# Decays of a chunkwise recurrence by half chunks, and a first product in two column parts

## Chip, cores, metric

One core of a Trainium2 chip. The metric is device time in microseconds of one execution of the kernel; the median of three runs stands for it.

## The reference

Four batches of eight heads run a gated recurrence over 768 steps with head size 40, and two dense layers follow it. Cut to what matters:

```python
for t in range(S):
    m_new = np.maximum(f_gate[:, :, t] + m, i_gate[:, :, t])
    f_stab = np.exp(f_gate[:, :, t] + m - m_new)
    i_stab = np.exp(i_gate[:, :, t] - m_new)
    C = f_stab * C + i_stab * outer(vt, kt)
    n = f_stab * n + i_stab * kt
    y[:, :, t] = sigmoid(o_gate) * (C @ qt) / max(abs(n @ qt), 1)
x = y as (3072 tokens, 320)
h = x @ w_in;  g = h - tanh(h);             x = g @ w_out
h = x @ w_in;  g = h, 0 or (h + 1)**2 / 4;  return g @ w_out
```

Each layer has 2048 hidden columns. Everything is float32.

## The kernel before

The recurrence is computed in chunks of 128 steps (L). A job n is one chunk of one batch: n = 4 * chunk + batch, so there are 24 jobs. For its eight heads, in two halves u of four heads, a job forms:

- d, the decay matrix: for every pair of steps (s, t) of the chunk the product of f over the steps between. VectorE makes it for a half with one tensor_tensor_scan (line 462) of 128x512: data0 is f of the four heads, broadcast over partitions, with a 0 at each head's first step; data1 is scan_id, the identity four times. For jobs 0 to 3 the broadcast is made by TensorE (t_f, line 453); from job 4 on (FIRST) it is a load, fb, from the scratch tensor fr_d.
- the scores k times q (t_s, line 475, and line 493 from job 12 on), and their product with d on VectorE (line 497).
- t_n: q times the carried state C (line 524) plus d times V (line 533). V is scaled by i on GpSimd (line 504), K by the last column of d, copied by ScalarE into wc (lines 465, 510).
- the output x: t_n over its denominator, times the output gate (lines 540 to 558), three transposes t_x on TensorE (line 562) and the copy into the layer's operand (xf for jobs 0 to 3, line 598).
- the new state: K times V (t_c, line 569), and C (line 586).

The gates run for all 32 heads at once in five groups of chunks. `decays` finishes a group: the running product gr (line 389), a 0 at each chunk's first step (line 392), and the writes of f and gr to scratch memory.

The layers work on blocks of four jobs, 512 tokens. A step is one of 16 groups of 128 hidden columns: first product (line 651 for steps 0 to 7 of block 0, in plain f32 and called wide; line 661 else), activation, second product (line 713). Steps of one block and jobs of the next are interleaved. The weights of layer 1 arrive as 64-bit words and are rebuilt by ScalarE and VectorE (lines 322 to 335).

The order on every engine is made by a planner, the class Plan. Each operation has an engine, a cost, a priority and the buffers that it reads and writes; a list scheduler sets the order, and each engine then runs its instructions in that order. Where the planner sees TensorE idle ahead of step 0 it puts in filler products into a spare bank (line 807). The operations that the prediction follows are these:

```python
op("DVE", dve(1024), p, lambda o=dk[u][0], i=f[u][0]: nc.vector.tensor_tensor_scan(
    out=o(), data0=i(), data1=scan_id, initial=0.0, op0=ALU.mult, op1=ALU.add), [f[u][1], "scan_id"], [dk[u][1]], lock=n >= FIRST)
```

Of the kernel before, what the change touches and what calls it, by code (L numbers as in the profile page):

```python
# [18 lines left out]
L = 128  # L19
# [18 lines left out]
FIRST = BLK[0]  # L38

# [10 lines left out]
WIDE = 8  # L50
W_LATE = 15
# [24 lines left out]
class Plan:  # L76
# [10 lines left out]
    def __init__(self):  # L87
        self.ops, self.tags, self.last, self.read = [], {}, {}, {}
        self.warm, self.end_warm, self.filler, self.gate, self.more = True, None, None, None, {}
# [33 lines left out]
    def schedule(self):  # L123
# [32 lines left out]
        while done < len(self.ops):  # L156
# [44 lines left out]
            done += 1  # L201
        self.ops.sort(key=lambda o: (o.start, o.seq))
# [30 lines left out]
def mlstm_moe_moe(ctx: ExitStack, tc: tile.TileContext, ig, fg, qk, qk3, q3, nat, w1, w2, cst, out):  # L233
# [11 lines left out]
    scan_bf = scan_id.bitcast(BF16)  # L245
# [5 lines left out]
    fr_d = dram.tile([NC, B * H, L], F32, name="fr_d")  # L251
# [129 lines left out]
    def decays(g, prio):  # L381
# [5 lines left out]
        for c in range(cb - ca):  # L387
            if ca + c:
                op("DVE", dve(2 * L), prio + 0.1 * c, lambda c=c: nc.vector.tensor_tensor_scan(
                    out=gr[:, c * L:(c + 1) * L], data0=fr[0:32, c * L:(c + 1) * L], data1=zero, initial=1.0,  # L390
                    op0=ALU.mult, op1=ALU.add), [(fr, c), "zero"], [gr])
            op("DVE", 60, prio + 0.1 * c, lambda c=c: nc.vector.memset(fr[0:32, c * L:c * L + 1], 0.0), [(fr, c)], [(fr, c)])
        z = slice(n - L, n)
        load(max(prio, -60), lambda: fr_d[cb - 1], lambda: fr[0:32, z], 16, [(fr, cb - ca - 1)], [("fr_d", g)], rows=512)
        load(max(prio, -60), lambda: gr_d[cb - 1], lambda: gr[:, z], 16, [gr], [("gr_d", g)], rows=512)
# [12 lines left out]
    def job(n, at, ld):  # L408
# [15 lines left out]
        f = {}  # L424
        if n >= FIRST:
            for u in range(2):
                ft = abuf("fb", [128, HU, L], F32, 2)
                load(ld + 0.5, lambda ft=ft: ft.t.rearrange("p h t -> p (h t)"), lambda u=u: fr_d[
                    c, b * H + u * HU:b * H + (u + 1) * HU].rearrange("h t -> (h t)").unsqueeze(0).to_broadcast([128, HU * L]),
                    256, r=[("fr_d", kc)], w=[ft], rows=512, margin=1200 if n >= 8 else 0.0)  # L430
                f[u] = lambda ft=ft: ft.t.rearrange("p h t -> p (h t)"), ft
# [12 lines left out]
        dk = {}  # L444
        d0 = wbuf(6 + n % 2, [128, 1024], F32, "d0") if n < FIRST else None
        wc = abuf("wc", [128, H], F32, 2)
        for u in range(2):
            p = at(0) if u == 0 else at(1)
            if n < FIRST:
                ft = jbank(n, "f", "t_f")  # L450
                for h in range(HU):
                    r = b * H + u * HU + h
                    op("PE", 2 * pe(L, 128, 2), p, lambda h=h, r=r, ft=ft: nc.tensor.matmul(  # L453
# [490 lines left out]
```

## Time and profile before

| what | value |
|---|---|
| median of 3 runs | 807.09 us (806.79 to 807.47) |
| the profiled execution | 807.17 us, span 805.4 us |
| TensorE busy | 798.4 us, 99% of the span |
| VectorE, ScalarE, GpSimd busy | 566.4, 426.3, 145.1 us |
| granted TensorE clock | 1.0 throughout |

The span runs from the first to the last instruction; the rest of the execution lies around it. Busy time is the union of the instructions' records; a product's record can contain waiting, since products are pipelined.

### The profile page before, as it was taken

To read this page: it belongs to the slowest core of one execution; us is meant where nothing else is said; L and a number is where in the kernel's file an instruction comes from. 1 tells how busy PE (TensorE), PEld (TensorE's weight loads), DVE (VectorE), ACT (ScalarE), POOL (GpSimd) and SP (SyncE) were. 2 spreads that over 40 slices of the span, in tenths; PEclk is the share of its full clock that TensorE was granted. 3 is DMA by queue.
4 is the path that set the end of the run, shared out by engine and by line. 5 is a ranking of instruction groups with operands and counts; after the bars stand their busy time and mean duration, and the time that the engine had idled before them with its cause. 6 is when DMAs were issued, how large, how long until landed. Compare 5 with 4: busy or idle time off the path is not lost.

```text
span 805.4 us, 15259 instructions
## 1 busy us (share of the span) xinstructions
PE 798.4 (99%) x6029; PEld 693.3 (86%) x6029; DVE 566.4 (70%) x924; ACT 426.3 (53%) x810; POOL 145.1 (18%) x146
## 2 busy tenths in 40 slices
PE   9999999999999999999999999999999999999998
PEld 7666888888988989898899898888889889898887
DVE  7999998988887897887466674645546465564644
ACT  4966876566586657554455543534435344342533
POOL 3142233213225234332100200200200101000000
PEclk9999999999999999999999999999999999999999
DMA  8979356676668576771543310100100000000000
GB/s 281 326 225 308 104 178 178 180 246 188 174 172 260 163 213 165 228 217 64 145 133 91 93 34 1 40 33 1 47 26 1 33 1 1 33 1 1 34 1 33
DMA packets 47619, 93.66 MB, mean 116 GB/s; under 512 B 4700, under 2 KB 25020, under 8 KB 47548
## 3 DMA queue, kind: packets, MB, share of 16 engines
q1 hardware_dynamic: 47500, 92.66, 38.8%
q8 instruction: 47, 0.77, 0.4%
q14 instruction: 24, 0.20, 0.1%
q10 hardware_dynamic: 48, 0.03, 0.0%
HBM read 78.88 MB, written 13.80 MB: 115 GB/s over the span
## 4 chain that ended last, share of the span: by engine, by line
PE 95%; DVE 2%; DMA 1%; SPq 0%; issue 0%; ACT 0%; POOL 0%; POOLq 0%; DVEq 0%; ACTq 0%
PE a L713 41%; PE h L661 38%; PE h L651 3%; PE t_n L533 2%; PE h L640 2%; PE t_n L524 2%; PE t_s L475 1%; PE t_c L569 1%; PE t_s L493 1%; PE t_x L562 1%; PE t_f L453 1%; PE spare L807 1%; DMA nat<-in_nat_dram 1%; DVE d L462 1%; SPq L287 0%
## 5 line engine op out<-in xcount | busy, mean ns | idle before, releaser
L661 PE MATMUL h<-x,w 128*128 128x512 f32 x1376 | 340.6, 396 | 0.0
L713 PE MATMUL a<-w,gh 128*128 128x320 f32 x1472 | 328.4, 310 | 0.0
L661 PEld LDWEIGHTS h<-x,w 128*128 128x128 f32 x1376 | 251.6, 188 | 55.2 <-issue 6.9
L713 PEld LDWEIGHTS a<-w,gh 128*128 128x128 f32 x1472 | 248.7, 188 | 8.0 <-ACT ob L736 1.8
L713 PE MATMUL a<-w,gl 128*128 128x320 f32 x736 | 228.2, 311 | 0.0
L684 DVE TENSOR_SCALAR g<-h 128x512 f32<-128x512 f32 x96 | 63.6, 684 | 115.9 <-PE h L661 115.9
L686 ACT ACTIVATE g<-g,half 128x512 f32<-128x512 f32 x96 | 66.9, 721 | 136.2 <-DVE g L684 135.7
L713 PEld LDWEIGHTS a<-w,gl 128*128 128x128 f32 x736 | 138.1, 188 | 0.4
L688 DVE TENSOR_TENSOR g<-h,g 128x512 f32<-128x512 f32 x96 | 64.6, 692 | 27.7 <-ACT g L686 26.9
L692 ACT CAST gh<-g 128x512 fp32r<-128x512 f32 x96 | 59.5, 623 | 43.1 <-DVE g L688 39.8
L680 DVE TENSOR_TENSOR h<-h,g 128x512 f32<-128x512 f32 x88 | 60.9, 693 | 26.8 <-ACT g L679 26.3
L679 ACT ACTIVATE g<-h 128x512 f32<-128x512 f32 x88 | 52.6, 598 | 46.6 <-PE h L661 46.2
L693 DVE TENSOR_TENSOR gl<-h,gh 128x512 fp32r<-128x512 f32 x88 | 59.9, 684 | 20.1 <-ACT gh L692 19.1
L777 POOL TENSOR_TENSOR x<-xl,x 128x512 fp32r<-128x512 f32 x18 | 24.8, 1398 | 271.2 <-ACT x L768 270.7
L692 ACT CAST gh<-h 128x512 fp32r<-128x512 f32 x88 | 51.4, 585 | 40.5 <-DVE h L680 25.4
L693 DVE TENSOR_TENSOR gl<-g,gh 128x512 fp32r<-128x512 f32 x96 | 61.9, 686 | 2.9
L462 DVE TENSOR_TENSOR_SCAN d<-fb,scan_id 128x512 f32<-128x512 f32 x40 | 52.8, 1326 | 2.0 <-DMA fb<-fr_d 1.8
L490 POOL TENSOR_TENSOR xf<-qkraw,xf 120x1024 fp32r<-120x1024 f32 x12 | 29.6, 2467 | 79.5 <-ACT xf L488 48.3
L488 ACT ACTIVATE xf<-qkraw,cs 120x512 fp32r<-120x512 f32 x48 | 32.7, 718 | 15.7 <-PE t_s L493 10.7
L497 DVE TENSOR_TENSOR d<-t_s,d 128x512 f32<-128x512 f32 x48 | 31.8, 680 | 4.6 <-PE t_s L493 2.4
L556 POOL TENSOR_TENSOR nat<-nat,dn 128x320 f32<-128x320 f32 x23 | 21.7, 944 | 69.6 <-DVE dn L542 67.7
L322 ACT ACTIVATE cvb<-w,half 128x704 bf16<-128x704 int8 x32 | 29.8, 932 | 2.1 <-DVE w L324 2.1
(105 smaller groups left out, 754.0 us busy)
## 6 DMA issues: line engine op xcount, KB each, us to landing
w<-in_w_dram SPq DMA_DIRECT2D x32, 703.6 KB
nat<-in_nat_dram SPq DMA_DIRECT2D x24, 484.0 KB
qkraw<-in_qk_dram SPq DMA_DIRECT2D x24, 480.0 KB
fb<-fr_d SPq DMA_DIRECT2D x40, 256.0 KB
w_d<-w SPq DMA_DIRECT2D x16, 352.0 KB
w<-w_d SPq DMA_DIRECT2D x16, 352.0 KB
qkraw<-in_qk_dram SPq DMA_DIRECT2D x24, 160.0 KB
xr_d<-xo SPq DMA_DIRECT2D x24, 160.0 KB
```

The lines of the kernel that those rows point to most:

```text
L462: op("DVE", dve(1024), p, lambda o=dk[u][0], i=f[u][0]: nc.vector.tensor_tensor_scan(out=o(), data0=i(), data1=scan_id, initial=0.0, op0=A ...
L488: op("ACT", act(512, 1), at(u - 1), lambda raw=raw, t=t, z=z, cols=cols: nc.scalar.activation(t[:, cols], raw[:, cols], AF.Copy, scale=cs[ ...
L497: op("DVE", dve(512), at(2 + u), lambda p=sp[u], d=dk[u][0]: nc.vector.tensor_tensor(out=d(), in0=p.t, in1=d(), op=ALU.mult), [sp[u], dk[u ...
L661: op("PE", pe(n), prio, lambda i=i, c=c, s=s: nc.tensor.matmul(p[:, :n], w[:, c:c + 128], x[:, s, :n], start=(i == 0 and not layer), stop= ...
L679: op("ACT", act(n), prio + 0.5 - FFN, lambda: nc.scalar.activation(t[:, :n], p[:, :n], AF.Tanh), [p], [t])
L680: op("DVE", dve(n), prio + 0.5 - FFN, lambda: nc.vector.tensor_tensor(out=p[:, :n], in0=p[:, :n], in1=t[:, :n], op=ALU.subtract), [p, t], [p])
L684: op("DVE", dve(n), prio + 0.5 - FFN, lambda: nc.vector.tensor_scalar(t[:, :n], p[:, :n], -1.0, 1.0, op0=ALU.max, op1=ALU.min), [p], [t])
L686: op("ACT", act(n, 1), prio + 0.5 - FFN, lambda: nc.scalar.activation(t[:, :n], t[:, :n], AF.Square, bias=half[:, 0:1], scale=0.5), [t, "h ...
L688: op("DVE", dve(n), prio + 0.5 - FFN, lambda: nc.vector.tensor_tensor(out=t[:, :n], in0=p[:, :n], in1=t[:, :n], op=ALU.max), [p, t], [t])
L692: op("ACT", act(n), prio + 1 - FFN, lambda: nc.scalar.copy(gh[:, :n], y[:, :n]), [y], [gh])
L693: op("DVE", dve(n), prio + 1 - FFN, lambda: nc.vector.tensor_tensor(out=gl[:, :n], in0=y[:, :n], in1=gh[:, :n].bitcast(F32), op=ALU.subtra ...
L713: op("PE", pe(DM) if gl is not None else 2 * pe(DM, 128, 2), prio, lambda A=A, r=r, a=a, c=c, i=i, dt=dt: nc.tensor.matmul(A[:, 0:DM], a[: ...
```

## The change

From job 4 on, the fifth job (n >= FIRST), a half's d is built from half chunks of 64 steps. d of a half is laid out as (second index half, head, 64 columns). One scan of 128x256 makes both diagonal blocks at once: rows 0 to 63 get f of the first half chunk, rows 64 to 127 of the second, and data1 is half_id, the 64x64 identity four times on each half of the rows. ScalarE copies the second diagonal block (rows 64 to 127) to the columns where it belongs, GpSimd sets the rows it leaves to zero, and the block between the halves (rows 0 to 63, later columns) is a GpSimd product of the first block's last column with the running product inside the second half chunk, which `decays` makes with one more scan (pr). So fr_d has three parts per chunk, and fb is loaded in two pieces. half_id is written over scan_id by two GpSimd copies after job 3. Every product of d times V still has 128 rows.

In steps 0 and 1 the three first products are split into columns of jobs 0 to 2 (384) and of job 3 (128). The scores of job 0 are moved behind the first four products of t_f; one filler is added ahead of them.

```diff
@@ decays
+                pr = abuf("pr", [B * H, HL], F32, 1)
+                op("DVE", dve(L), prio + 0.1 * c, lambda m=m: nc.vector.tensor_tensor_scan(
+                    out=pr.t, data0=fr[0:32, m:m + HL], data1=zero[:, 0:HL], initial=1.0,
+                    op0=ALU.mult, op1=ALU.add), [*f, "zero"], [pr])
...
-        load(max(prio, -60), lambda: fr_d[cb - 1], lambda: fr[0:32, z], 16, [(fr, cb - ca - 1)], [("fr_d", g)], rows=512)
+        for u, a in ((0, z), (2, z + HL)):
+            load(max(prio, -60), lambda u=u, a=a: fr_d[cb - 1, u], lambda a=a: fr[0:32, a:a + HL], 8, [(fr, cb - ca - 1)], [("fr_d", g, u)], rows=256)
+        load(max(prio, -60), lambda: fr_d[cb - 1, 1], lambda: pr.t, 8, [pr], [("fr_d", g, 1)], rows=256)
@@ job: loads of fb
-                ft = abuf("fb", [128, HU, L], F32, 2)
...
-                    256, r=[("fr_d", kc)], w=[ft], rows=512, margin=1200 if n >= 8 else 0.0)
+                ft = abuf("fb", [128, 2 * HU * HL], F32, 2)
+                for a, w, kb in ((0, 2, 128), (HL, 1, 64)):
+                    load(ld + 0.5, lambda ft=ft, a=a, w=w: ft[a:a + HL, 0:w * HU * HL].rearrange("p (w x) -> p w x", w=w),
...
@@ job: d
-            op("DVE", dve(1024), p, lambda o=dk[u][0], i=f[u][0]: nc.vector.tensor_tensor_scan(
-                out=o(), data0=i(), data1=scan_id, initial=0.0, op0=ALU.mult, op1=ALU.add), [f[u][1], "scan_id"], [dk[u][1]], lock=n >= FIRST)
+            op("DVE", dve(512), p, lambda o=dk[u][0], i=f[u][0]: nc.vector.tensor_tensor_scan(
+                out=o()[:, 0:HU * HL], data0=i(), data1=half_id, initial=0.0, op0=ALU.mult, op1=ALU.add),
+               [*f[u][1], ("half_id", 0), ("half_id", HL)], [A, Z], lock=True)
+            op("ACT", act(256), p + 0.3, lambda ds=ds: nc.scalar.copy(ds()[HL:128, 1], ds()[HL:128, 0]), [Z], [D_C])
+            op("POOL", 300, p + 0.4, lambda ds=ds: nc.gpsimd.memset(ds()[HL:128, 0], 0.0), [], [Z])
+            op("POOL", pool(256), p + 0.3, lambda ds=ds, i=pb[u][0]: nc.gpsimd.tensor_tensor(
+                out=ds()[0:HL, 1], in0=i(), in1=ds()[0:HL, 0, :, HL - 1:HL].to_broadcast([HL, HU, HL]), op=ALU.mult),
+               [A, pb[u][1]], [D_B], lock=True)
@@ scores of job 0
+            if n == 0:
+                P.more[o] = 1
+                P.behind.append((o, bc[HU - 1]))
@@ step, wide
+            cut = BLK[0] - 1 if f < SPLIT else 0
+            for a, b in ((0, cut), (cut, BLK[0])) if cut else ((0, BLK[0]),):
+                for i in range(3):
+                    op("PE", 2 * pe((b - a) * L, 128, 2), prio, lambda i=i, z=slice(a * L, b * L): nc.tensor.matmul(
+                        p[:, z], w[:, i * 128:(i + 1) * 128].bitcast(F32), x[:, i, z], start=(i == 0), stop=(i == 2)),
+                       [w, *((x, m) for m in range(a, b))], [p])
@@ after jobs(0)
+    for a in (0, HL):
+        op("POOL", 400, JOB0 + 12, lambda a=a: nc.gpsimd.tensor_copy(
+            half_id[a:a + HL].rearrange("p (h t) -> p h t", t=HL), ident[a:a + HL, a:a + HL].unsqueeze(1).to_broadcast([HL, HU, HL])),
+           ["cs"], ["scan_id", ("half_id", a)])
```

Here SPLIT is 2 and HL is 64. The planner orders every later job anew. Three places show it; rows of the change carry its own line numbers.

TensorE, before, from the last transposes of stage 1 to step 0 (t_x is line 562, step 0's products are line 651; six fillers stand ahead of these rows, behind job 3's d times V):

```order
L807 LDWEIGHTS gh
L807 MATMUL spare<-gh 128x512
L562 MATMUL t_x<-cs,x 128x128 x3
L807 LDWEIGHTS gh
L807 MATMUL spare<-gh 128x512
L807 LDWEIGHTS gh
L807 MATMUL spare<-gh 128x512
L807 LDWEIGHTS gh
L807 MATMUL spare<-gh 128x512
L651 MATMUL h<-xf,wf 128x512 x9
```

The same place now, from job 3's d times V (line 575 of the change; t_x is 604, the wide steps are 695):

```order
L575 MATMUL t_n<-nat,d_389 32x41 x32
L695 MATMUL h<-xf,wf 128x384 x3
L604 MATMUL t_x<-cs,x 128x128 x3
L695 MATMUL h<-xf,wf 128x384 x2
L695 MATMUL h<-xf,wf 128x128 x3
L695 MATMUL h<-xf,wf 128x384
L695 MATMUL h<-xf,wf 128x128 x3
L695 MATMUL h<-xf,wf 128x512 x3
```

The nine fillers are gone, and products of steps 0 and 1 stand around the transposes.

GpSimd at the end of stage 1 and at job 4, before (504 scales V, 510 K, 556 the output gate, 514 and 516 q):

```order
L510 TENSOR_TENSOR nat<-nat,wc 128x320 x2
L556 TENSOR_TENSOR nat<-nat,dn 128x320
L514 TENSOR_TENSOR q_632<-q_632,gb 120x256
L516 TENSOR_TENSOR q_632<-q_632,gb 80x128
L504 TENSOR_TENSOR nat<-nat,isT 128x328
```

Now (552 is the old 510, 598 the old 556, 546 the old 504, 556 and 558 the old 514 and 516; 876 makes half_id, 500 is the product and 499 the zeros of job 4):

```order
L552 TENSOR_TENSOR nat<-nat,wc 128x320
L876 COPY scan_id<-cs 64x256 x2
L552 TENSOR_TENSOR nat<-nat,wc 128x320
L598 TENSOR_TENSOR nat<-nat,dn 128x320
L546 TENSOR_TENSOR nat<-nat,isT 128x328
L500 TENSOR_TENSOR d<-fb,d 64x256
L499 MEMSET d 64x256
L556 TENSOR_TENSOR q_638<-q_638,gb 120x256
L499 MEMSET d 64x256
L558 TENSOR_TENSOR q_638<-q_638,gb 80x128
L500 TENSOR_TENSOR d<-fb,d 64x256
```

The copies stand between the scalings of K, and the second half's product of job 4 stands behind q's scaling.

VectorE at job 4, before (613 and 617 split x, 675 the activation, 324 and 326 weights; a scan is printed as SCALAR_TENSOR_TENSOR):

```order
L613 TENSOR_TENSOR x_634<-xf,x_634 128x1024
L462 SCALAR_TENSOR_TENSOR d<-fb,scan_id 128x512 x2
L497 TENSOR_TENSOR d<-t_s,d 128x512 x2
L675 TENSOR_TENSOR gh<-h,g 128x512
L324 TENSOR_TENSOR w_617<-w_617,cvb 128x704
```

Now (495 is the scan, 539 the old 497, 655 the old 613, 719 the old 675, 331, 333 and 342 weights):

```order
L495 SCALAR_TENSOR_TENSOR d<-fb,scan_id 128x256 x2
L539 TENSOR_TENSOR d<-t_s,d 128x512
L333 SCALAR_TENSOR_TENSOR wf<-w_531,wf 128x704
L331 TENSOR_TENSOR w_631<-w_631,cvb 128x704
L333 SCALAR_TENSOR_TENSOR w_631<-w_555,w_631 128x704
L719 TENSOR_TENSOR gh<-h,g 128x512
L342 TENSOR_TENSOR w_723<-w_631,w_723 128x704
L539 TENSOR_TENSOR d<-t_s,d 128x512
L495 SCALAR_TENSOR_TENSOR d<-fb,scan_id 128x256
L655 TENSOR_TENSOR x_660<-xf,x_660 128x1024
```

The scans come ahead of the split of x, and the second half's product with the scores stands five instructions behind the first's.

## Rows read from the trace of the kernel before

**Rows 1.** The page's engines: busy us (share of the span) xinstructions

```profile
PE 798.4 (99%) x6029; PEld 693.3 (86%) x6029; DVE 566.4 (70%) x924; ACT 426.3 (53%) x810; POOL 145.1 (18%) x146
```

**Rows 2.** Windows: length, busy us of PE, PEld, DVE, ACT, POOL, PEclk, DMA, GB/s

```profile
28.00:31.10 3.10, 2.59 (x24) 1.08 (x12) 2.54 (x6) 2.63 (x7) 0.00 (x0) 1.00 1.01 403
...
40.00:120.00 80.00, 80.00 (x735) 61.27 (x733) 74.62 (x120) 55.52 (x112) 25.48 (x26) 1.00 0.65 203
120.00:390.00 270.00, 268.24 (x2509) 240.20 (x2509) 226.30 (x384) 167.37 (x354) 84.86 (x83) 1.00 0.65 183
```

**Rows 3.** Chain of waits, stage 1 to step 0: start us, us, what

```profile
14.04 1.82 PE t_f L453 x16
...
27.36 0.79 PE t_n L533 x64
...
29.38 0.50 DVE x L553
...
30.02 0.52 PE t_x L562 x3
30.54 0.65 PE spare L807 x3
31.19 7.91 PE h L651 x18
```

**Rows 4.** Timeline, job 0: start us, us, engine, instruction, [idle before, releaser]

```profile
4.99 1.61 PE L475 MATMUL t_s<-qkraw 40*128 40x128 f32 x16
...
8.03 2.34 DVE L462 TENSOR_TENSOR_SCAN d<-t_f,scan_id 128x512 f32<-128x512 f32 x2 [0.93 <-PE t_f L453]
```

**Rows 5.** Timeline, end of stage 1, VectorE and GpSimd

```profile
23.41 0.87 DVE L326 SCALAR_TENSOR_TENSOR wf<-w,wf 128x704 int32<-128x704 int32 x1
...
24.00 0.87 POOL L510 TENSOR_TENSOR nat<-nat,wc 128x320 f32<-128x320 f32 x1 [2.59 <-ACT wc L465]
...
25.67 0.48 DVE L558 TENSOR_TENSOR x<-t_n,nat 128x320 f32<-128x320 f32 x1
```

**Rows 6.** Groups by line: xcount | busy us, mean ns | idle before us, releasers

```profile
L462 DVE TENSOR_TENSOR_SCAN d<-fb,scan_id 128x512 f32<-128x512 f32 x40 | 52.8, 1326 | 2.0 <-DMA fb<-fr_d 1.8
...
L524 PE MATMUL t_n<-C,q 120*128 120x123 f32 (+1 forms) x120 | 16.4, 271 | 0.7 <-POOL nat L504 0.7
...
L562 PE MATMUL t_x<-cs,x 128*128 128x128 f32 x72 | 11.8, 273 | 1.4 <-DVE x L558 0.9 <-DVE x L553 0.5
...
L612 ACT CAST x<-t_x 128x256 fp32r<-128x256 f32 x20 | 7.5, 374 | 8.2 <-PE t_x L562 8.1
...
L797 POOL COPY scan_id<-cs 128x512 f32<-128x512 f32 x1 | 0.7, 746 | 1.2 <-DMA cs<-in_cst_dram 1.2
...
L810 POOL MEMSET gh<- 128x512 f32 x1 | 0.5, 524 | 0.3 <-POOLq L931 0.3
...
L389 DVE TENSOR_TENSOR_SCAN gate<-gate,zero 32x128 f32<-32x128 f32 x1 | 0.4, 407 | 0.2 <-issue 0.2
```

**Rows 7.** One line's instructions: xcount, ns min/median/max, first and last start us

```profile
L514 POOL TENSOR_TENSOR q<-q,gb x20: 732/751/1668, 43.0 to 373.6; 120x256 f32<-120x256 f32 x20
...
L510 POOL TENSOR_TENSOR nat<-nat,wc x20: 714/723/868, 10.9 to 305.1; 128x320 f32<-128x320 f32 x20
...
L462 DVE TENSOR_TENSOR_SCAN d<-fb,scan_id x40: 1172/1215/2182, 44.9 to 372.6; 128x512 f32<-128x512 f32 x40
```

**Rows 8.** Timeline, job 5's scans beside GpSimd

```profile
52.70 2.77 DVE L462 TENSOR_TENSOR_SCAN d<-fb,scan_id 128x512 f32<-128x512 f32 x2
...
52.87 1.52 POOL L556 TENSOR_TENSOR nat<-nat,dn 128x320 f32<-128x320 f32 x1 [3.70 <-DVE dn L542]
```

**Rows 9.** Timeline, jobs 9 and 10: a scan that waits for its load

```profile
130.51 1.23 DVE L462 TENSOR_TENSOR_SCAN d<-fb,scan_id 128x512 f32<-128x512 f32 x1 [1.76 <-DMA fb<-fr_d]
...
131.76 0.34 SPq L287 DMA_DIRECT2D fb<-fr_d  x1
...
133.22 0.87 PE L524 MATMUL t_n<-C,q 120*128 120x123 f32 x6 [0.69 <-POOL nat L504]
```

More of the change, by code (lines that the diff above doesn't have):

```diff
@@ L88, in __init__ @@
         self.ops, self.tags, self.last, self.read = [], {}, {}, {}
-        self.warm, self.end_warm, self.filler, self.gate, self.more = True, None, None, None, {}
+        self.warm, self.end_warm, self.filler, self.gate, self.more, self.behind = True, None, None, None, {}, []
     def buf(self, pool, shape, dtype, tag, name, cap=1):
@@ L201, in schedule @@
             done += 1
+        for o, first in self.behind:
+            if o.start <= first.start:
+                after = min((x for x in self.ops if x.eng == o.eng and (x.start, x.seq) > (o.start, o.seq)), key=lambda x: (x.start, x.seq))
+                after.fill, o.fill = after.fill + o.fill, 0
+                o.start = first.start + 0.5
         self.ops.sort(key=lambda o: (o.start, o.seq))
@@ L244, in mlstm_moe_moe @@
     scan_id = const.tile([128, 512], F32, name="scan_id")
-    scan_bf = scan_id.bitcast(BF16)
+    half_id = scan_id[:, 0:HU * HL]
     isT = const.tile([128, NC, B * H], F32, name="isT")
@@ L461, in job @@
                 dk[u] = lambda u=u: d0[:, u * 512:(u + 1) * 512], (d0, u)
-            op("DVE", dve(1024), p, lambda o=dk[u][0], i=f[u][0]: nc.vector.tensor_tensor_scan(
-                out=o(), data0=i(), data1=scan_id, initial=0.0, op0=ALU.mult, op1=ALU.add), [f[u][1], "scan_id"], [dk[u][1]], lock=n >= FIRST)
+            pk[u] = [dk[u][1]]
+            if n < FIRST:
+                op("DVE", dve(1024), p, lambda o=dk[u][0], i=f[u][0]: nc.vector.tensor_tensor_scan(
+                    out=o(), data0=i(), data1=scan_id, initial=0.0, op0=ALU.mult, op1=ALU.add), [f[u][1], "scan_id"], [dk[u][1]], lock=n >= FIRST)
+                if not last:
+                    op("ACT", 200, p + 0.3, lambda u=u, i=dk[u][0]: nc.scalar.copy(
+                        wc[:, u * HU:(u + 1) * HU], i().rearrange("p (h t) -> p h t", t=L)[:, :, L - 1]), [dk[u][1]], [(wc, u)])
+                continue
+            ds, k = lambda o=dk[u][0]: o().rearrange("p (s h t) -> p s h t", s=2, t=HL), dk[u][1]
+            A, Z, D_B, D_C = pk[u] = [(k, x) for x in "azbc"]
+            op("DVE", dve(512), p, lambda o=dk[u][0], i=f[u][0]: nc.vector.tensor_tensor_scan(
[6 more added lines that the diff above has]
+               [A, pb[u][1]], [D_B], lock=True)
             if not last:
-                op("ACT", 200, p + 0.3, lambda u=u, i=dk[u][0]: nc.scalar.copy(
-                    wc[:, u * HU:(u + 1) * HU], i().rearrange("p (h t) -> p h t", t=L)[:, :, L - 1]), [dk[u][1]], [(wc, u)])
+                op("ACT", 200, p + 0.4, lambda u=u, ds=ds: nc.scalar.copy(
+                    wc[:, u * HU:(u + 1) * HU], ds()[:, 1, :, HL - 1]), [D_B, D_C], [(wc, u)])
         sp = [jbank(n, f"s{u}", "t_s") for u in range(2)]
@@ L497, in job @@
             op("DVE", dve(512), at(2 + u), lambda p=sp[u], d=dk[u][0]: nc.vector.tensor_tensor(
-                out=d(), in0=p.t, in1=d(), op=ALU.mult), [sp[u], dk[u][1]], [dk[u][1]])
+                out=view(d()), in0=view(p.t, True), in1=view(d()), op=ALU.mult), [sp[u], *pk[u]], pk[u])
         K, V, O = (nt, 0), (nt, 1), (nt, 2)
```

45 lines of the change are left out of this document (26 added, 19 removed).

## The prediction

> **What bounds the kernel now.** I read the page's table of engines first: TensorE is busy for 99% of the span, and VectorE, the next, for 70% [rows 1]. That share says little alone, because a product that waits can count as busy. So the second view is a table of windows [rows 2]. Between 40 and 120 us VectorE works 74.62 of 80 us, nearly as much as TensorE; between 120 and 390 us it has 226.30 of 270; GpSimd has 84.86 of 270 there. In the 3.1 us before the wide steps begin TensorE works 2.59 us, and the next view shows that much of this is not work of the task.
>
> The third view is the chain of waits around that place [rows 3]. TensorE finishes job 3's d times V at 27.36 + 0.79 = 28.15 us. VectorE then scales job 3's output; its last product ends at 29.38 + 0.50 = 29.88, TensorE transposes x at 30.02, ScalarE copies it into xf, and only at 31.19 does the first product of step 0 begin. Between 28.15 and 31.19 TensorE does one useful thing, three transposes; the rest are filler products (line 807) into a spare bank, nine of them. From 31.19 on it hardly stands: over the whole run its idle time ahead of transposes of x is 1.4 us (0.5 of that in stage 1, behind VectorE's line 553) and ahead of q times C 0.7 us [rows 6]. So after 31.19 only 0.9 + 0.7 = 1.6 us is visible waiting. What starts TensorE's steps earlier ends the run earlier, unless a new wait gives it back; what relieves VectorE or ScalarE is worth at most those 1.6 us.
>
> **Part 1, the first product in two column parts.** Step 0's product over columns of jobs 0 to 2 (384 of 512) needs nothing of job 3. In the changed order three such products stand directly behind job 3's d times V, with job 3's transposes behind them. A 512-column f32 product is two passes; 18 passes take 7.91 us, 0.439 each [rows 3]. By columns a pass of 384 takes 0.330; a pass of 128 columns (another f32 product, the broadcast of f) takes 1.82 / 16 = 0.114 [rows 3]. The new course from 28.15: six passes of 384, to 30.13; the transposes of job 3, whose x is ready at 29.88, so they no longer wait, with the 0.52 of the row, to 30.65; four passes of step 1 at 0.330, to 31.97; six of 128 for step 0, to 32.65 (they need xf of job 3, which was there at 31.19 after transposes at 30.02 and so comes about 31.3 now); two of 384, to 33.31; six of 128, to 33.99. Step 2 thus starts at 33.99, against 31.19 + 12 x 0.439 = 36.46 before: **2.47 us earlier**. The two parts cost 6 x (0.330 + 0.114) = 2.66 us where a whole step costs 2.63, which the course already contains. The fillers that go are the cover that goes with them: if x of job 3 comes late, TensorE simply stands.
>
> **Part 2, the copies that make half_id.** Two GpSimd copies now stand in its queue between two scalings of K (lines 510), behind the last scan of stage 1. A 128x512 copy took 0.746 [rows 6], so 64x256 is about 0.4, twice 0.8. They start when VectorE's last stage-1 scan ends, where line 326 runs from 23.41 to 24.28 [rows 5]. If they may run beside it, they end at 24.3, 0.3 later than the 24.00 at which line 510 began. If they must wait for it, they end near 25.1; line 510 and then line 556 come to 26.5, and VectorE's line 558 ends at 27.0 instead of 26.15. The two weight conversions behind it would then delay job 3's chain by about 0.6. The bounds are 0 and 0.6; I take **0.4**, since the nearest pair of rows shows such a wait: line 556 took 1.52 us, where its median is near line 510's 0.723, while it lay under a scan [rows 7, 8].
>
> **Part 3, scores of job 0 behind the gates.** VectorE's first scan waited 0.93 us for the broadcast, which stood behind these sixteen passes and their 1.61 us [rows 4]. Now four products of the broadcast come first. The scan gains about 1 us, but the second scan still needs the second four, which follow the scores; and job 1's scores and broadcast follow the same total of work on TensorE. An added filler of 0.65 / 3 = 0.22 us [rows 3] takes its place in a wait. I cost it at **0**, between -0.25 and +0.25.
>
> **Part 4, decays by half chunks.** Forty scans of 128x512, 1.326 us in the mean [rows 6] and 1.215 in the median [rows 7], become 128x256. No such row exists; a scan of 128 columns on 32 partitions took 0.407 [rows 6], so a line through 0.407 and 1.215 puts 256 at about 0.67. VectorE saves 40 x 0.54 = 21.6 us. Four more scans of 64 columns in the later gate groups take it at most 0.4 each, and the fifth runs at 5 us beside other waits. ScalarE gains forty 64x256 copies at 0.37 (its 128x256 copy [rows 6]), 15 us on an engine with slack. GpSimd gains forty products, between 0.62 (0.723 for 320 columns, scaled) and 0.751 for 256 columns [rows 7], and forty memsets at about 0.26 (half of 0.524 [rows 6]): 25 to 30 us plus 10 in a stretch where it works under a third of the time. None of this is on TensorE's path except through d: a half's path was one scan of 1.215 and is now 0.67 + 0.62 to 0.75 + a handover, so 0.1 to 0.3 longer, mostly long before the scores are there.
>
> The shared resource matters more than the counts. Where line 556 lay under two scans it took 1.52 us, and two scans took 2.77 [rows 8]: two such operations don't run side by side. The forty products take that path for about what the shorter scans give back, 25 against 21.6 us. The Trainium skill, SBUF — State Buffer, section "Who interferes with whom", says the pair of ports is an exclusive lock between a VectorE operation with two SBUF inputs and a GpSimd operation that reads SBUF, and that one that only writes does not contend. The first half agrees with these rows (1.52 against 0.72); by the second half the memsets cost no port, which no row here shows; if they did, 10 us of port time would be added, beside other work.
>
> SyncE gets 40 more loads of fb (two per half, 192 KB instead of 256) and ten more writes of fr. An issue takes 0.34 us of its queue [rows 9]. I cost them at nothing on the path, since none of the 1.6 us of TensorE's later waits is put down directly to a load [rows 6]. If that cover goes, a late fb is the price: the scan of job 10 waited 1.76 us for fb, VectorE's queue stood behind it, and TensorE lost 0.69 [rows 9]. fb's two buffers are now held until the GpSimd product is done, up to 1 us longer. Against that, scans are shorter. For later waits I take **-0.3**, between -1.6 (all visible ones go) and +2.5 (three or four more like job 10's).
>
> **Sum.** -2.47 + 0.4 + 0 - 0.3 = -2.4. The profiled execution took 807.17 us (span 805.4), the median is 807.09, 0.08 less. So 807.09 - 2.4 = **804.7 us**.
>
> **Rivals.**
> A. VectorE's relief counts: it is the engine packed between 40 and 120 us, and the later waits run through its queue. Then the 1.6 us of visible waits and the small ones go, and the copies of part 2 cost nothing: 807.1 - 2.5 - 1.6 = 803.0, down to 802.2. Against it: the order of every later job is new, so waits are drawn anew.
> B. Late loads or late halves: some of the twenty jobs meet what job 10 met. Two to three waits of 0.7 on top of the forecast give 806.1 to 806.9. The gain that starts at 28 us would also be smaller if xf of job 3 comes late, since ScalarE works 2.63 of 3.10 us there [rows 2]; then only the six passes ahead of the transposes count, about 1.3 of the 2.47, and 805.9 is left.
> C. Slower: the GpSimd link sets d in every job. It decides when the product, in order behind GpSimd's other work (a split of q and k there, or q's scaling that waits for its load) or locked out by a scan, ends after the scores. With 0.33 us late in each of twenty jobs 6.6 us are lost and the time is 807.1 - 2.4 + 6.6 = 811; it turns slower by over 0.2% (1.6 us, about what a measurement here can tell from no change) from 4.0 us on, 0.2 a job. Against it: most first-half scans now end many us ahead of the scores, and GpSimd is two thirds idle. The Trainium skill, GPSIMD Engine Reference, section "4.1 Engine selection", advises against just this: elementwise products of two inputs belong on VectorE, GpSimd taking about twice as long. The rows agree in direction (0.62 to 0.75 against 0.54 saved per half); here the rule's loss falls on an idle engine.
>
> **How the numbers follow.** The forecast (803.9 to 805.4) has 0.45, A 0.20, B 0.27, C 0.08. The range 802.2 to 807.2 takes in the forecast, A and B, and leaves out C and the tails. Faster by over 0.2% means below 805.5: the forecast and A, 0.65. Within it: B, 0.27. Slower: C, 0.08.
>
> **What would show it.** In the changed profile the first 384-column product should start near 28.2 (28.6 with part 2's delay), job 3's transposes should come directly behind, no filler should lie after 28, and step 2 should start at about 34.0 to 34.4. Scans should take about 0.67, GpSimd's products 0.6 to 0.75 with some at 1.3 or more. TensorE's layer 2 should begin as much earlier as the steps did. I am wrong if the first wide product starts at 29 or later, if idle time ahead of TensorE's t_n or t_x lines exceeds 4 us, or if VectorE's busy time doesn't fall by some 20 us.

## The result, and the profile after

The changed kernel takes **813.5 us** in the median of six runs (811.8 to 814.73), the kernel before in the same session 806.95: a ratio of 1.0073, 95% interval 1.0061 to 1.0084. It is 6.5 us slower, where 2.4 us faster was forecast. Its profiled execution, the fastest of the six, took 811.8 us, with a span of 810.0 and a granted clock of 1.0, so its trace shows 4.6 of the 6.5 us.

The page's engines, chain by engine and two groups, of the changed kernel (the scan of half chunks is line 495, GpSimd's product 500):

```profile
PE 799.1 (99%) x6033; PEld 692.9 (86%) x6033; DVE 549.2 (68%) x929; ACT 444.5 (55%) x850; POOL 181.8 (22%) x228
...
PE 87%; DMA 6%; DVE 2%; issue 2%; ACT 1%; POOL 1%; SPq 1%; POOLq 0%; DVEq 0%; ACTq 0%
...
L500 POOL TENSOR_TENSOR d<-fb,d 64x256 f32<-64x256 f32 x40 | 28.6, 722 | 13.8 <-DVE dn L583 3.3
L495 DVE TENSOR_TENSOR_SCAN d<-fb,scan_id 128x256 f32<-128x256 f32 x40 | 29.5, 748 | 2.8 <-DMA fb<-fr_d 2.7
```

Against [rows 1] VectorE loses 17.2 us of work, GpSimd gains 36.7 and ScalarE 18.2. The scans cost 29.5 us instead of 52.8 [rows 6], so the relief is there, and nothing came of it. The chain that ended last runs through loads for 6% of the span, in the kernel before for 1%. About half of that lies in stage 1, ahead of 28 us; behind it stand the load of nat shown further down and these three, where the chain of the kernel before has one load:

```profile
121.90 4.44 DMA fb<-fr_d
...
195.82 3.88 DMA fb<-fr_d
...
205.58 7.29 DMA gb<-gr_d
```

The windows of [rows 2], now:

```profile
28.00:31.10 3.10, 3.10 (x73) 1.85 (x71) 2.71 (x7) 2.21 (x7) 0.00 (x0) 1.00 0.89 303
40.00:120.00 80.00, 79.46 (x668) 60.71 (x667) 71.68 (x123) 62.05 (x123) 29.94 (x42) 1.00 0.67 191
120.00:390.00 270.00, 265.36 (x2548) 235.74 (x2547) 210.49 (x381) 177.78 (x381) 116.04 (x147) 1.00 0.63 180
```

Between 120 and 390 us TensorE now stands for 4.64 us, where it stood for 1.76 [rows 2], and between 40 and 120 us for 0.54 instead of 0. TensorE's timeline, stage 1's end and the largest later waits (695 is the wide first product, 604 the transposes, 566 q times C):

```profile
27.80 0.55 PE L604 MATMUL t_x<-cs,x 128*128 128x128 f32 x3
28.27 0.82 PE L575 MATMUL t_n<-nat,d 128*32 128x41 f32 x64
29.02 2.20 PE L695 MATMUL h<-xf,wf 128*128 128x384 f32 x6
31.23 0.52 PE L604 MATMUL t_x<-cs,x 128*128 128x128 f32 x3
31.59 3.44 PE L695 MATMUL h<-xf,wf 128*128 128x384 f32 x18
35.62 2.84 PE L695 MATMUL h<-xf,wf 128*128 128x512 f32 x6 [0.60 <-DVE gh L719]
...
131.51 0.69 PE L514 MATMUL t_s<-qkraw 40*128 40x128 f32 x7 [0.60 <-PE h L705]
...
185.86 0.87 PE L566 MATMUL t_n<-C,q 120*128 120x123 f32 x6 [1.71 <-issue]
...
216.08 0.52 PE L604 MATMUL t_x<-cs,x 128*128 128x128 f32 x3 [0.55 <-DVE x L600]
...
218.77 0.64 PE L535 MATMUL t_s<-xf 120*128 120x128 f32 x4 [0.64 <-DVE x L659]
```

The column parts stand where they should, without fillers, and step 2 begins at 35.62 instead of about 36.4. But a wait stands ahead of it that the prediction did not have. Followed by the count of layer products done, a rough measure since the two orders interleave jobs and steps differently, the changed kernel is 0.6 us ahead at 72 us, 1.4 behind at 160, 3.3 at 187, and 4.5 from 400 us to the end: all is lost while jobs and steps are interleaved. The largest piece, by the chain of waits around 185.86 (550 is the sigmoid of the output gate, 723 a tanh, 498 ScalarE's copy of the lower right block):

```profile
175.61 5.84 DMA nat<-in_nat_dram
...
182.81 0.02 ACT nat L550
...
183.19 0.58 ACT g L723
...
183.80 0.41 ACT d L498
```

The load of nat lands at 181.45. ScalarE's queue stands behind it, with a table load of 1.28 us ahead of the sigmoid, and VectorE's score product (line 539, at 185.06) behind ScalarE. That TensorE stands behind this product is not in the profile, which names no releaser, but in the program: t_n is written into the bank of the first half's scores. So two questions: which part of the change costs this, and by which mechanism.

One caution on single profiles: kernels with the same instructions in stage 1 (the kernel before, and patience_160 below) have job 3's transposes at 30.0 and at 31.6 us; 1.0 us of this arose at the start, where the first fillers and score products took 5.2 us in the one execution and 6.2 in the other. So I compare medians, and within a trace stretches that begin at the same operation.

### The profile page after: what moved, and what is told of

The parts are those of the page before. It is cut to its first block, busy times and chain, and to the rows that moved or that the text cites. A ratio compares the mean times of both kernels' runs of the same rounds, so it can differ in the third digit from the quotient of the medians.

```text
span 810.0 us, 15587 instructions
## 1 busy us (share of the span) xinstructions
PE 799.1 (99%) x6033; PEld 692.9 (86%) x6033; DVE 549.2 (68%) x929; ACT 444.5 (55%) x850; POOL 181.8 (22%) x228
## 4 chain that ended last, share of the span: by engine, by line
PE 87%; DMA 6%; DVE 2%; issue 2%; ACT 1%; POOL 1%; SPq 1%; POOLq 0%; DVEq 0%; ACTq 0%
PE a L757 39%; PE h L705 37%; DMA w<-in_w_dram 2%; PE h L682 2%; PE h L695 2%; PE t_n L575 2%; DMA nat<-in_nat_dram 2%; PE t_n L566 1%; PE t_s L535 1%; DMA fb<-fr_d 1%; PE t_c L611 1%; PE t_s L514 1%; DMA gb<-gr_d 1%; PE t_x L604 1%; SPq L294 1%
## 5 line engine op out<-in xcount | busy, mean ns | idle before, releaser
L546 POOL TENSOR_TENSOR nat<-nat,isT 128x328 f32<-128x328 f32 x24 | 20.2, 850 | 66.7 <-DMA nat<-in_nat_dram 44.6
L500 POOL TENSOR_TENSOR d<-fb,d 64x256 f32<-64x256 f32 x40 | 28.6, 722 | 13.8 <-DVE dn L583 3.3
L495 DVE TENSOR_TENSOR_SCAN d<-fb,scan_id 128x256 f32<-128x256 f32 x40 | 29.5, 748 | 2.8 <-DMA fb<-fr_d 2.7
```

## Experiments

### Which part costs it

In half_only the split and the moved scores are taken back (SPLIT = 0, no `behind`); the other three put parts into the kernel before:

(The diffs below are shortened.)

```diff
half_only:   -SPLIT = 2   +SPLIT = 0   and without P.more[o] = 1; P.behind.append(...)
split_only:  before, with the new loop over column parts, SPLIT = 2
behind_only: before, with P.more[o] = 1; P.behind.append((o, bc[HU - 1]))
no_half:     before, with both
```

> The change without the column parts and with the scores of job 0 where they were: only the decays by half chunks are left. Theory 1 (the half-chunk decays bring the lost time: their loads are issued late and their GpSimd product and ScalarE copy stand in queues on which later waits of TensorE end): 811 to 813 us, with idle time of TensorE near 130, 186 and 216 us as in the change. Theory 2 (stage 1 is what costs: the copies, the filler and the split steps set every later job off the plan): 807 us within 1. Theory 3 (any new order of the jobs draws new waits, whichever part makes it): between 806 and 813, with waits in other places than those of the change.

> The kernel before with nothing but the column parts. Step 2's product needs the bank that step 0's activation frees; in the change it waited 0.6 us for that. If that bank bounds it, step 2 starts about 1.0 to 1.5 us earlier than the 36.3 us of before (not 2.5), and by theory 1 the whole is 805.4 to 806. Theory 2: no earlier than 807. Theory 3: 804 to 809.

> The kernel before with nothing but the scores of job 0 behind the first half of the broadcast, and the added filler. If the filler and the order push job 1's broadcast back as in the change (11.04 against 10.48 us), 807.2 to 807.7 us by theories 1 and 2; by theory 3 the later order may add or take up to 2 us.

> The kernel before with the column parts of steps 0 and 1 and with the scores of job 0 behind the gates; decays as before. Theory 1: about 805.5 to 806.5 us, the split's 1 to 1.5 us less the 0.5 us that the moved scores and the filler cost job 1. Theory 2: 811 to 813. Theory 3: anywhere from 804 to 810, with waits of TensorE in new places.

| run | median, us | against before (807.53) | ratio, 95% interval |
|---|---|---|---|
| half_only | 812.26 | +4.7 | 1.0048 to 1.0072 |
| split_only | 814.31 | +6.8 | 1.0071 to 1.0097 |
| behind_only | 808.12 | +0.6 | 0.9994 to 1.0012 |
| no_half | 815.75 | +8.2 | 1.0088 to 1.012 |

The half chunks alone cost 4.7 us and the split alone 6.8, all together 6.5: they don't add. no_half came out above every range set for it, split_only above those of theories 1 and 3. split_only touches six products at 28 us, but TensorE's largest waits are those of 1.6 us at 119 and 2.7 at 148 us. That speaks for the order that the planner laid out anew. VectorE, GpSimd and TensorE there, in split_only (357 is a scan of the gates, 491 GpSimd's share of the split of q and k, 696 VectorE's subtraction for gl):

```profile
144.14 3.55 DVE L357 TENSOR_TENSOR_SCAN mg<-fr,carry,ig 32x128 f32<-32x128 f32 x1
147.62 0.65 DVE L696 TENSOR_TENSOR gl<-h,gh 128x512 fp32r<-128x512 f32 x1
```

```profile
143.69 0.72 POOL L557 TENSOR_TENSOR nat<-nat,dn 128x320 f32<-128x320 f32 x1
144.38 0.72 POOL L511 TENSOR_TENSOR nat<-nat,wc 128x320 f32<-128x320 f32 x1
145.05 2.36 POOL L491 TENSOR_TENSOR xf<-qkraw,xf 120x1024 fp32r<-120x1024 f32 x1
```

```profile
148.32 0.96 PE L664 MATMUL h<-x,w 128*128 128x512 f32 x3 [2.71 <-DVE gl L696]
```

The small scan takes 0.466 us in the median of its four in this trace (0.47 to 1.51 in the kernel before); here it ends 0.3 us after GpSimd's three products, 3.55 us after its start. gl stands behind it, and TensorE 2.71 us behind gl. This agrees with the Trainium skill, SBUF — State Buffer, section "Who interferes with whom", by which VectorE with two SBUF inputs and GpSimd reading SBUF exclude each other.

The loss doesn't end with the wait. Behind it TensorE's granted clock was 0.5, the lower of its two levels (1.2 GHz), from 149.7 to 153.1 us (a window as in [rows 2]):

```profile
149.80:153.10 3.30, 3.30 (x14) 2.81 (x14) 2.58 (x5) 0.53 (x2) 0.00 (x0) 0.50 0.86 257
```

So the 6.8 and 8.2 us of split_only and no_half contain some clock: their runs have means of 0.994 to 0.998. The changed kernel's six have 0.999 or 1.0, so the clock is no part of its 6.5 us.

### The same parts with the old order kept

The planner is run on the old operations; the new instructions are put in afterwards. For the half chunks they are tied to the scan:

```diff
+P.side.append((o, "ACT", 700, copy)); P.side.append((o, "POOL", 705, product)); P.side.append((o, "POOL", 710, memset))
+for o, eng, late, fn in self.side: e.start = o.start + late
```

For the column parts, the 384-column products get `e.start = self.tx.start - 0.5`, tx being job 3's transposes. patience_160 is the kernel before with one number changed: `-PATIENCE = 150.0 +PATIENCE = 160.0`.

> Only the column parts, with the order of the kernel before kept: the planner is run on the old whole products, and afterwards the six 384-column products are put in by hand ahead of job 3's transposes (the fillers there go, the 128-column products stand where the whole ones stood; every other row of every engine stands as before). Theory 'new order' (the column parts alone cost 6.8 us because the planner laid out all later jobs anew): what is left is the local gain of stage 1, bounded by the wait for a bank of PSUM that the changed kernel shows at 35.62 us, so about -0.8 us against before (between -1.6 and +0.4), and no wait of 1 us or more on TensorE between 100 and 160 us where the planner's version had 1.8 and 2.9. Theory 'the parts themselves cost' (stage 1, the banks): +4 to +7 us again.

> Only the half-chunk decays, with the order of the kernel before kept: the planner is run on the old whole scans and one load of fb per half, and afterwards ScalarE's copy, GpSimd's product and memset of each half are put in beside the scan, both parts of fb are issued where the one load stood, both scans of gr and pr where the one stood. TensorE's rows are the same as before, one by one. Theory 'new order': the 4.7 us of half decays go, and what is left is the path through GpSimd and ScalarE and the extra issues, -0.3 to +1.5 us. Theory 'half decays cost' (later fb, GpSimd link, 40 copies on ScalarE): +3.5 to +6 us again, with the waits in front of t_n and t_x.

> Both of the two runs above in one kernel. 'New order': the sum of both effects, about -1 to +1 us, so far under the +6.5 of the changed kernel. If each part costs by itself: +6 us or more.

> The kernel before with one number of the planner changed, by which an operation may be put ahead of another that could start 160 ns sooner instead of 150: nothing is computed otherwise, the same operations stand on each engine, in another order from job 4 on. 'New order' (the order of before is one with few waits on the chip; another of the planner's orders draws more): slower by 1 to 9 us, with waits on TensorE that put themselves down to VectorE's, ScalarE's or a load's lateness at places where before has none. The other theories: within 0.5 us of before.

| run | median, us | against before (807.14) | ratio, 95% interval |
|---|---|---|---|
| split_kept | 809.73 | +2.6 | 1.0022 to 1.0045 |
| half_kept | 816.36 | +9.2 | 1.0094 to 1.0127 |
| both_kept | 819.92 | +12.8 | 1.0137 to 1.0165 |
| patience_160 | 811.54 | +4.4 | 1.0038 to 1.0063 |

patience_160 bears out the theory of the order: nothing is added, and 4.4 us are lost. But it doesn't explain everything, as half_kept shows: with TensorE's rows the same as before, the half chunks cost 9.2 us, and parts now add (2.6 + 9.2 against 12.8). My theory fell for them; their operations cost time by themselves. And split_kept was not a fair copy: I had put six products ahead of job 3's transposes, where the change has three. ScalarE's copy of xf then came at 32.87 instead of 30.57, the weight conversions and step 0's tanh behind it, and TensorE stood 3.23 us for the bank. Behind that its granted clock was 0.5 again, from 39.7 to 43.1 us:

```profile
38.23 4.10 PE L663 MATMUL h<-xf,wf 128*128 128x512 f32 x6 [3.23 <-DVE gh L690]
```

```profile
39.70:43.00 3.30, 3.30 (x6) 1.56 (x5) 2.28 (x4) 1.88 (x4) 0.00 (x0) 0.50 0.83 235
```

The six passes took 4.10 us where split_one, below, has 2.84, and the second products behind them 2.80 instead of 2.32. Three of split_kept's six runs have a mean clock of 1.0 and still took 809.25 to 809.79 us.

What such an order draws, in patience_160 (326 is a conversion of weights, 490 GpSimd's split):

```profile
143.44 2.99 DVE L326 SCALAR_TENSOR_TENSOR w<-w,w 128x704 int32<-128x704 int32 x1
```

```profile
142.97 2.71 POOL L490 TENSOR_TENSOR xf<-qkraw,xf 120x1024 fp32r<-120x1024 f32 x1 [2.02 <-ACT xf L488]
```

```profile
148.44 1.64 PE L661 MATMUL h<-x,w 128*128 128x512 f32 x6 [0.81 <-DVE gl L693]
```

A conversion that elsewhere takes 0.89 us takes 2.99 beside GpSimd. The order decides which operation meets that.

### The bank behind the column parts; the links and loads of the half chunks

```diff
split_one:     split_kept with -SPLIT = 2 +SPLIT = 1
split_lift:    split_one, +P.lift += [(tanh, 2), (subtract, 1)] for steps 0 and 1
half_no_link:  half_kept, -POOL memset(Z) +ACT activation(Z, copy, scale=0.0); rows 0 to 63 of wc copied by POOL
half_one_load: half_kept, -2 loads of 64 rows +1 load [2 blocks x 64 rows x 512] per half
```

> As the run split_kept (order of the kernel before kept, parts put in by hand), but only step 0 is cut, so only three products of 384 columns (2.2 us) stand ahead of job 3's transposes, which then come about 0.5 us later than before and not 2.3. Theory 'bank': TensorE's step 0 and step 1 end 1.3 us earlier, but step 2 needs the bank that VectorE's subtraction of step 0 frees at about 35.9 us (behind ScalarE's conversions and tanh, which came no earlier), so nearly nothing is left: -0.6 to +0.6 us against before, with a wait for VectorE's gh in front of step 2 of about 1 us. Theory 'the new copy of xf held ScalarE up in split_kept': the +2.6 us of that run go, same number. Theory of the prediction (products set the time there): -1.3 us with no wait.

> split_one, and the tanh (ScalarE) and subtraction (VectorE) of steps 0 and 1 each moved ahead of the weight conversions that stood directly before them in their queues (two rows on ScalarE, one on VectorE); nothing else changes. Theory 'bank': the bank is free at about 34.5 us, step 2 starts 1 to 1.4 us earlier than before, and TensorE keeps it where no later wait takes it: -1.4 to -0.4 us against before. If the conversions were due (they end late for steps 3 to 6), the gain is lost there: 0 to +1 us.

> As the run half_kept, but no engine waits for the other within a half: ScalarE itself writes the zeros (a copy scaled by 0) behind its copy of the lower right block, so GpSimd's memset and its wait for ScalarE go, and the lower 64 rows of wc are copied by GpSimd behind its product, so ScalarE's copy of wc no longer waits for GpSimd. Theory 'links' (queues of GpSimd and ScalarE stand behind those waits, and q times g, t_c and x behind them): a good part of half_kept's +9.2 us goes, +2 to +5 left. Theory 'loads' (fb in two parts takes SyncE's queue and brings gb and nat late): +8 to +9.5 us as before, waits for gb and nat remain.

> As the run half_kept, but fb of a half comes in one load again (256 KB, the fourth block unused; 2 issues per job and not 4), from a layout of fr in memory by head groups; fr is written in four parts per group. Theory 'loads': a good part of half_kept's +9.2 us goes, +2 to +5 left, and the waits behind gb and nat go. Theory 'links': +8 to +9.5 us as before.

| run | median, us | against before (807.29) | ratio, 95% interval |
|---|---|---|---|
| split_one | 807.19 | -0.1 | 0.9987 to 1.0004 |
| split_lift | 806.84 | -0.5 | 0.9988 to 1.0005 |
| half_no_link | 817.54 | +10.2 | 1.0107 to 1.0138 |
| half_one_load | 934.92 | +127.6 | 1.1567 to 1.1602 |

VectorE's subtraction of step 0, which frees the bank, in the kernel before; then TensorE in split_one and in split_lift:

```profile
35.22 0.68 DVE L675 TENSOR_TENSOR gh<-h,g 128x512 f32<-128x512 f32 x1
```

```profile
30.10 0.49 PE L570 MATMUL t_x<-cs,x 128*128 128x128 f32 x3
...
36.03 2.84 PE L663 MATMUL h<-xf,wf 128*128 128x512 f32 x6 [1.36 <-DVE gh L690]
```

```profile
31.68 0.49 PE L588 MATMUL t_x<-cs,x 128*128 128x128 f32 x3
32.01 0.81 PE L843 MATMUL spare<-gh 128*128 128x512 bf16 x3
32.74 6.14 PE L681 MATMUL h<-xf,wf 128*128 128x128 f32 x18
38.72 2.32 PE L749 MATMUL a<-wf,gh 128*128 128x320 f32 x8
```

The theory of the bank holds. In the kernel before the bank was free at 35.9 us and step 2 began at about 36.4, so no more than 0.5 us was to be had. split_one ends its products early and then stands 1.36 us. With tanh and subtraction ahead of the conversions the wait is gone: from job 3's transposes to the first second product (line 713 before) pass 7.04 us, where split_one takes 8.61 (38.71 - 30.10) and the kernel before 8.92 (38.94 - 30.02 [rows 3]). Of these 1.9 us the median keeps 0.5, which can't be told from nothing: in the trace of split_lift 0.8 us are lost again at 49 us, where TensorE waits for GpSimd's scaling of q; a wait of 0.86 at 134 us has a like of 0.69 in the kernel before [rows 9]. This is the best version of the study, no faster than before within its interval.

half_no_link gave nothing back; it takes a wait away, but adds forty copies to ScalarE, so it doesn't acquit the links. half_one_load doesn't answer its question: the one load of two blocks is itself slow, TensorE stood long, and its mean granted clock was 0.943. Its chain of waits, in which a load stands from issue to landing:

```profile
34.73 17.09 DMA fb<-fr_d
...
54.13 16.02 DMA fb<-fr_d
...
71.64 14.13 DMA fb<-fr_d
```

Over its whole chain such a load takes 10.5 to 17.1 us, in the changed kernel's chain 3.9 to 4.4.

### Issues, GpSimd's queue, other orders

```diff
fb_parts:          before, each load of fb as 2 loads of 64 partitions x 512
half_old_load:     half_kept, with the write of fr and the loads of fb as before
after_160:         the changed kernel, -PATIENCE = 150.0 +PATIENCE = 160.0
patience_140:      before, -PATIENCE = 150.0 +PATIENCE = 140.0
half_old_load_dve: half_old_load, -gpsimd.tensor_tensor(product) +vector.tensor_tensor(product) behind the scan
half_dve:          half_kept, the same
```

half_old_load and half_old_load_dve leave out the new factors: their scans, copies and products run on the values of the old load.

> The kernel before, in its own order, with each load of fb issued as two loads of 64 partitions and 512 columns instead of one of 128: the same bytes, four issues per job on SyncE's queue instead of two, nothing else. In half_kept the issues of fb take 51.3 us of SyncE's queue instead of 14.5 (80 at 0.64 us against 40 at 0.36). Theory 'issues' (everything behind them in SyncE's queue, gb, q and nat above all, comes later): a good part of half_kept's +9.2 us appears here, +3 to +9. Theory 'work of GpSimd and ScalarE': within 1 us of before.

> half_kept with the write of fr and the loads of fb as in the kernel before (one write, one load of 128x512 per half): the short scans, ScalarE's copies, GpSimd's products and memsets all stay and run on these values, which are not the factors that they need, so the decays d of jobs from five on come out other than the reference's. Theory 'issues': most of the +9.2 us goes, 0 to +4 left. Theory 'work of GpSimd and ScalarE': +6 to +9.5 stays.

> The changed kernel with the planner's patience at 160 ns instead of 150, which lays out another order of the same operations. Theory 'one unlucky order': between 0 and +12 us against before, at least 1.5 us away from the changed kernel's +6.5. If the cost lies in the operations themselves: +5.5 to +7.5.

> The kernel before with the planner's patience at 140 ns instead of 150: the same operations in another order from stage 1 on. Theory 'the order of before is one with few waits': slower, +1 to +9 us (patience_160 gave +4.4). If orders don't differ much: within 1 us of before.

> half_old_load with each half's product of 64x256 on VectorE directly behind its scan instead of on GpSimd; the memset stays on GpSimd behind ScalarE's copy. As there, the loads are the old ones and d of jobs from five on comes out other than the reference's. Theory 'GpSimd's queue': the waits at 58, 121 and 235 us (0.95, 1.3 and 0.98 us) shrink or go, and of the +3.6 us +0.5 to +2 is left (a scan and a product take VectorE about 1.1 us, so nothing is won there either). If ScalarE's copies or the half_id copies are the cause: +3 to +4 stays.

> half_kept with each half's product on VectorE directly behind its scan; loads in two parts as in the change, the output is the reference's. Theory 'GpSimd's queue and the loads each have their share': +9.2 falls by 2 to 4 us, to +5 to +7. If GpSimd's queue alone is behind the rest too: below +3.

| run | median, us | against before (807.56; last two 807.50) | ratio, 95% interval |
|---|---|---|---|
| fb_parts | 810.08 | +2.5 | 1.0022 to 1.004 |
| half_old_load | 811.17 | +3.6 | 1.0032 to 1.0056 |
| after_160 | 818.2 | +10.6 | 1.0097 to 1.0136 |
| patience_140 | 808.71 | +1.2 | 1.0003 to 1.0021 |
| half_old_load_dve | 810.35 | +2.9 | 1.0021 to 1.0042 |
| half_dve | 815.01 | +7.5 | 1.0057 to 1.012 |

Both theories on the half chunks have a share. The issues alone, at the same bytes, cost 2.5 us. The loads of fb as one line's instructions, in the kernel before and in half_kept:

```profile
L287 SPq DMA_DIRECT2D fb<-fr_d x40: 326/349/430, 33.5 to 355.4; - x40
```

```profile
L450 SPq DMA_DIRECT2D fb<-fr_d x80: 451/603/1622, 35.1 to 363.9; - x80
```

Forty issues of 0.35 us have become eighty of 0.60 in the one queue through which gb, q, nat and the weights also come. In fb_parts the eighty take 0.587 in the median, so its queue is held nearly as long.

Without new loads 3.6 us are left, and the trace of half_old_load has them in one view. GpSimd, then TensorE, at 118 us (497 is the half's product, 496 the memset, 495 ScalarE's copy, 548 and 550 scale q):

```profile
118.37 0.31 POOL L496 MEMSET d<- 64x256 f32 x1 [0.38 <-ACT d L495]
118.75 0.62 POOL L497 TENSOR_TENSOR d<-fb,d 64x256 f32<-64x256 f32 x1
120.14 0.31 POOL L496 MEMSET d<- 64x256 f32 x1 [0.77 <-ACT d L495]
120.52 0.73 POOL L548 TENSOR_TENSOR q<-q,gb 120x256 f32<-120x256 f32 x1
121.21 0.46 POOL L550 TENSOR_TENSOR q<-q,gb 80x128 f32<-80x128 f32 x1
```

```profile
121.31 0.90 PE L558 MATMUL t_n<-C,q 120*128 120x123 f32 x6 [0.76 <-POOL q L548]
```

d itself is not late. The scaling of q is, because it stands in GpSimd's queue behind a memset that waits for ScalarE. At 58 and 235 us the scaling of a job's output stands behind a product and a memset, and TensorE's transposes behind that. TensorE's rows are those of the kernel before, so how far it falls behind can be followed product by product: by 1.0, 1.3 and 1.0 us at these three places, and by 0.5 up to 39 us, the half_id copies included. That is 3.8; smaller losses of 1.6 and a gain of 2.0 at 134 and 293 us, where the kernel before has waits of its own, leave 3.4 in this trace. With the product on VectorE 2.9 are left: the losses at 58 and 235 us shrink to 0.5 and 0.8, the one at 121 stays, since the memsets are still in the queue. The two intervals overlap, so that this step helps is likely, not shown; the same holds for half_dve (+7.5) against half_kept (+9.2), where a fall to +5 to +7 was expected.

2.5 and 3.6 make 6.1 of the 9.2. half_kept and half_old_load differ only in the loads of fb and the writes of fr, so the other 3 us belong to these too, beside the new work; no run takes them apart further. By the count of products half_kept falls 1.4 us further behind at 149 us and 1.9 at 187, where half_old_load loses nothing and 0.3. At 187 us q's scaling waited for gb and then took 1.31 instead of 0.73, and TensorE stood behind it:

```profile
185.67 1.31 POOL L552 TENSOR_TENSOR q<-q,gb 120x256 f32<-120x256 f32 x1 [1.80 <-DMA gb<-gr_d]
```

```profile
187.03 0.71 PE L562 MATMUL t_n<-C,q 120*128 120x123 f32 x4 [1.66 <-POOL q L552]
```

Three orders of the old work have now been seen, before 807, patience_140 808.7 and patience_160 811.5, and two of the changed work, 813.5 and, with 160, 818.2. Of after_160's 10.6 us a part is clock: its one run with a mean of 1.0 took 813.52 us, the others 815.1 to 818.8 at 0.996 to 0.999. The order of before is the fastest of its three; three are too few to say what an order costs in the mean.

## Why the prediction was wrong

Of the prediction's own signs of being wrong one came: the first wide product started at 29.02 us. VectorE's busy time fell by 17.2 us, and the idle time ahead of t_n and t_x stayed at 3.1 us, under the 4 named.

- **Part 1**, -2.47: wrong. The step that failed is "Step 2 thus starts at 33.99". Two banks serve the wide first products, so step 2 needs what VectorE's subtraction of step 0 frees, and that stood in the kernel before at 35.22 to 35.90 behind ScalarE's and VectorE's conversions. I followed TensorE's products and the copy of xf, not who holds the bank. Measured: 35.62 in the changed kernel. Of the 1.63 us between, 0.60 is the wait for the bank and 0.87 the later start of the first wide product in this execution (29.02, not 28.15). In the old order with the wait for the bank cured, the products do come 1.9 us earlier (split_lift).
- **Part 2**, +0.4: right. In half_old_load, in the old order, from job 2's transposes to job 3's pass 3.37 us and from job 1's 8.60, against 3.15 and 8.19. The copies took 1.36 us together, not 0.8. They began behind the last scan of stage 1, at 23.67, beside the conversion, and VectorE's product for job 2 ended at 27.04, where the slower branch has 27.0.
- **Part 3**, 0: not refuted (behind_only +0.6, interval -0.5 to +1.0).
- **Part 4**, -0.3, at most +2.5: the step that cost most. It put the loads at nothing, "since none of the 1.6 us of TensorE's later waits is put down directly to a load"; fb_parts prices the issues at 2.5 us. It took VectorE's shorter scans as a gain on the path; they weren't on it. And it took the later waits from the trace of one order, while the change lays out another. With no work changed, other orders cost 1.2 and 4.4 us; the bound of +2.5 had no row under it for that. The memsets and ScalarE's copies were counted as work on engines with slack; what they cost is shown by half_old_load, 3.6 us with the products, through the operations queued behind them.
- **Rival C** gave the right side and nearly the time (811), by a mechanism that was half right. GpSimd did set the pace at three places of 1.0 to 1.3 us in half_old_load, but through q and the job output that stand behind the half's work, not through d in each of twenty jobs. That its time comes near is luck: the 0.33 us a job was supposed, and the cost arose elsewhere. Its chance of 0.08 was too small: the sentence against A, that the order of every later job is new and waits are drawn anew, held against the forecast itself.
- The relief of VectorE came as worked out: scans 0.69 us in the median of half_kept against the estimated 0.67, GpSimd's product 0.617, the memset 0.307. Sizes of instructions were right; what they stand in front of was not.

The shares in the changed kernel itself are shown only as far as this: the half chunks alone, laid out by the planner, cost 4.7 us; the split alone costs 6.8 in the order that the planner makes of it, and its first half (step 0) nothing in the old order (split_one); the two together cost 6.5 in a third order. Which of its waits belong to the operations and which to that order can't be said wait by wait.

## What to carry to other kernels

Before costing an operation that starts earlier, list what the next step on its engine needs besides operands: here a bank of PSUM, whose release lay one row away in VectorE's timeline. Where a planner sets the order, separate a change from the new order that it brings: run the old kernel with one harmless number of the planner changed to see what orders alone do, and put the change into the old order by hand. A small operation on an idle engine is priced by what stands behind it in that engine's queue, above all if it waits for another engine.

## What the runs showed of the hardware

- A VectorE scan of 32x128 took 3.55 us (split_only) instead of 0.466, and a conversion 2.99 (patience_160) instead of 0.89, while GpSimd worked through products of two SBUF inputs beside them. GpSimd's memsets took 0.305 to 0.309 us in all forty cases of the changed kernel, at least 14 of them beside VectorE operations with two SBUF inputs, so the one that only writes was not held up, as the Trainium skill, SBUF — State Buffer, section "Who interferes with whom", has it.
- A load whose source begins with a dimension of 2 (two blocks, each broadcast to 64 partitions) took 10.5 to 17.1 us from issue to landing in half_one_load's chain, where the changed kernel's loads of 64 partitions take 3.9 to 4.4. The Trainium skill, DMA: Bandwidth & Descriptors, section "Why a DMA increments its semaphore by 16 and not by 1", says that the slowest dimension of either side decides over how many DMA engines a copy is spread; with 2 it would be two of sixteen. The trace agrees: the 256 packets of a job's two such loads (39.5 to 51.3 us) ran two at a time for 10.5 of 11.8 us, while those of the kernel before ran up to 19 at a time and were through in 2.8 us. Which engines they ran on, the trace doesn't say.
- An issue of fb for 64 partitions took 0.60 us of SyncE's queue in the median (half_kept), for 128 partitions 0.35 (before). The two blocks aren't what makes it longer: the plain loads of 64 partitions in fb_parts took 0.587.
- TensorE's granted clock was at its lower level, 0.5, for 3.4 us after TensorE had stood 2.71 us (split_only) and 3.23 us (split_kept). Six passes of 512 columns and the eight second products behind them took 4.10 and 2.80 us there, and 2.84 and 2.32 at 1.0 (split_one).
